# Seven products instead of eight in the first matrix product from block 4 on, with a rewritten instruction list, in a fused retention and MLP kernel

## The chip, the cores and the metric

The kernel runs on one core of a Trainium2 chip. The metric is the device time of one execution in microseconds (us), start to end. The engines are TensorE (PE in the profile, with its weight loads as PEld), VectorE (DVE), ScalarE (ACT), GpSimd (POOL) and SyncE (SP). POOL and SP issue nearly all the transfers here.

## The reference

Inputs: q, k, v of shape (8, 8, 576, 64), that is batch B, heads H, positions S and head width D, and the MLP's weights `w_in` (512 x 2048) and `w_out` (2048 x 512), all float32. First a retention layer without softmax, then a GELU MLP over its 4608 tokens of width 512:

```python
scores = 1/sqrt(D) * q @ k.T                    # per batch and head
gamma  = 1 - 2.0 ** (-5 - arange(H))            # one decay per head
ret    = scores * where(rel >= 0, gamma ** rel, 0)   # rel = query position - key position
x      = (ret @ v) as (B*S, H*D)
out    = gelu(x @ w_in) @ w_out
```

## The kernel before

**Tiling.** The sequence of 576 is cut into four chunks of 128 positions and a tail of 64. A unit is one chunk of one batch; units 0 to 3 are the first chunks of batches 0 to 3, and from there two batches go side by side as a pair, so a group is a pair of units (or the two tails of a pair, in one unit). There are 36 units in 22 groups. For a group, q and k are turned (head width onto the partitions), scores are formed, masked by the decay, and multiplied by v (`inner`); the part from earlier chunks comes through a running state of keys times values (`state`, on the scaled v that `scaled_v` makes) and the turned q (`cross`); `evacuate` writes the result, transposed, into the MLP's input `xT`. Four units make a block of 512 tokens, so there are nine blocks, 0 to 8.

**The MLP.** Its first product for a block is 16 output stripes of 128, each four matmuls of 512 columns, in `mlp1` (line 762). For blocks 5 to 8 it is formed instead by `fast` (line 1021): on a pair of stripes, in four groups j of them, Strassen's method with seven products P1 to P7, each four matmuls of 256 columns (line 1047). The sums that it needs of the weights are made once, by `sum_in` and `sum_last` (the last writes over `w_in` itself, so no plain product may come after it), and those of the input once per block by `sum_x`. P7's product is copied out of PSUM into a tile `p7`, P1's is copied within PSUM, and sums on VectorE join the products. The second product of blocks 1 to 8 is made of seven products too, in `part` (line 948), with sums on VectorE of g and in `after`; block 0's is plain (`mlp2`, line 807).

**Buffers.** q and k of a group lie in one of `N_LD` = 5 load tiles. The turned q and k lie in one of `N_QKT` = 4 tiles; a turn into a tile waits until the cross product of the group four before has read it. The tile `p7` has no place of its own: up to block 6 it lies in the place of the mask `near`, then in a load tile.

**Turning.** `turn` (line 499) turns on TensorE through PSUM, four 128x128 transposes at a time; a full pair needs four such calls. `turn_dma` (line 510) has SP issue a DMA transpose from SBUF to SBUF, two per group. Groups 0 to 6 are turned on TensorE, groups 7 to 21 by DMA.

**The order of the work** is written out by hand in a list `SEQ` (line 1109), which `perform` goes through, and the framework keeps the order per engine. Each entry is a letter and numbers: L is a load (0, 1, 2 for q, k, v of a unit, 3 and 4 for a stripe of `w_in` and `w_out`), t a turn on TensorE, d a turn by DMA, s scores, m masking, i inner, u state, x cross, e evacuate, v scaling, 1 a call of `mlp1`, 2 of `mlp2`, f block.group.product of `fast`, p block.product.quarter of `part`, W, I, J, X and G the sums, K a late store, and w dummy matmuls on zeros that fill TensorE's time. Loads are issued by POOL in list order, at most eight in flight, over its software queue. DMA turns and output stores are issued by SP in list order, so a turn stands behind every store that comes ahead of it in the list, and a store waits for the last sum on VectorE that makes its rows. A planner in the same file keeps due times (`T`, `free_at`, `land`), and chooses by them between VectorE and ScalarE for copies and among PSUM banks; the list itself is fixed.

Of the kernel before, what the change touches and what calls it, by code (L numbers as in the profile page):

```python
# [9 lines left out]
FP32 = mybir.dt.float32  # L10
# [7 lines left out]
def kernel(  # L18
# [52 lines left out]
    FAST, ALL_FAST = 5, 5  # L71
    N_LD = 5
    N_QKT = 4
# [185 lines left out]

    def qk_free(n):  # L260
        g = groups[n]
        ends = list(sg[n]["ends"].values()) if "ends" in sg[n] else [sg[n]["T"]]
        assert len(ends) == 2 or n < N_PE_TR and sg[n]["halves"] == 4
        assert units[g[0]][2] is None or g[0] in s_done
        return max(ends + [st[g[0]].get("U", 0.0)])
# [141 lines left out]
    def pe_waits(until):  # L407
        assert until < 1e8
        T["pe"] = max(T["pe"], until)
# [109 lines left out]
    def scores(n):  # L519
        g = groups[n]  # L520
        qkT = sg[n]["qkT"]
        pe_waits(sg[n]["T"])
# [448 lines left out]
    near_p7 = True  # L971
# [5 lines left out]
    f_bank, f_at, f_done, f_begun, p7_tiles = {}, {}, {}, [], {}  # L977
# [43 lines left out]
    def fast(t, j, p):  # L1021
# [32 lines left out]
        elif p == P7:  # L1054
            late = t >= N_BLK - 2
            if late not in p7_tiles:
                more = {"tag": "qk", "bufs": N_LD} if late else {"tag": "near"}
                p7_tiles[late] = (ld_pool if late else const).tile([128, 2, 2, 256], FP32, name="p7", **more)
            f_bank[key, "p7"] = p7_tiles[late][:, j % 2]
# [45 lines left out]
    for _ in range(N_WARM):  # L1105
# [3 lines left out]
    SEQ = ("L3.1 L1.1 L3.0 L5.0 L0.1 L2.0 L0.2 L1.2 C0.0 C1.0 t0.0.0 Z0 w2 L2.1 Z0 Z1 t0.1.0 Z0 w5 L3.2 Z1 s0 m0 L2.2 Z1 "  # L1109
# [109 lines left out]
```

## Time and profile before

| what | value |
|---|---|
| time, median of 3 runs | 284.95 us (283.55 to 285.13) |
| the profiled execution | 284.17 us, span 282.3 us |
| TensorE busy | 276.3 us, 3413 matmuls |
| VectorE / ScalarE / GpSimd busy | 211.3 / 152.6 / 114.1 us |
| moved by DMA | 35.39 MB, software queue 18.10 MB, hardware queue 16.26 MB |
| output stores (256 KB) | 5.1 us from issue to landing (median) |
| DMA transposes | 30, 7.9 us from issue to landing (median) |

Reading the profile: the first page gives busy time per engine and the span in 40 slices; the chain of work runs backwards from the last instruction; the waits say which engine waited for whom. Matmuls overlap in the record, so a group's time in the chain (start to the next start) is its price, and the mean of one record is not.

### The profile page before, as it was taken

Reading aid. Unit: us, or ns where it says so; the run is one execution under the profiler, and the core shown is the slowest. Engines: PE = TensorE matmul, PEld = TensorE weight load, DVE = VectorE, ACT = ScalarE, POOL = GpSimd, SP = SyncE. Lnnn points to the kernel's source line nnn. Section 1 sums busy time; section 2 is a strip of 40 time slices with the busy share of each in tenths; the row PEclk is TensorE's granted clock in tenths of the full one; section 3 lists DMA queues with packets and bytes.
Section 4 is the critical chain, followed back from the end, with each engine's and each line's share of the span. In section 5 each row is a group of like instructions: output and inputs, shape, how many; then the busy total and the mean of one; then the engine's idle time right before and its main releaser. Section 6 shows DMA issues by size and latency. Waiting matters only on the chain.

```text
span 282.3 us, 8187 instructions
## 1 busy us (share of the span) xinstructions
PE 276.3 (98%) x3413; PEld 211.7 (75%) x3413; DVE 211.3 (75%) x413; ACT 152.6 (54%) x330; POOL 114.1 (40%) x143
## 2 busy tenths in 40 slices
PE   8999999999999999999999999999999999999994
PEld 3576777578874588547775588888888888888894
DVE  5662784886984775989749976898799989984852
ACT  5766745464156631575646565666584457765210
POOL 8987897907955447544076736000000000000000
PEclk9999999999999999999999999999999999999999
DMA  9999999999999999999999999960012013000035
GB/s 146 166 181 179 183 167 178 126 131 202 145 190 177 196 141 127 184 198 138 138 155 138 190 154 156 144 171 1 2 74 77 2 34 120 1 2 0 28 123 150
DMA packets 152804, 35.39 MB, mean 125 GB/s; under 512 B 141120, under 2 KB 148928, under 8 KB 152768
## 3 DMA queue, kind: packets, MB, share of 16 engines
q0 software_dynamic: 116832, 18.10, 101.2%
q1 hardware_dynamic: 34528, 16.26, 32.3%
q10 hardware_dynamic: 1408, 0.52, 0.8%
q8 instruction: 26, 0.43, 0.6%
q14 instruction: 10, 0.08, 0.1%
HBM read 36.70 MB, written 9.44 MB: 163 GB/s over the span
## 4 chain that ended last, share of the span: by engine, by line
PE 91%; POOL 4%; DMA 3%; issue 0%; DVE 0%; POOLq 0%
PE psum L948 35%; PE psum L762 23%; PE psum L1047 18%; PE psum L807 5%; PE psum L651 3%; PE psum L551 3%; DMA w_in<-in_moe_w_in_dram 3%; POOL qk L347 2%; PE psum L702 2%; PE psum L672 1%; POOL v_ld L347 1%; POOL w_in L306 1%; PE psum L499 1%; PE psum L538 0%; PE psum L637 0%
## 5 line engine op out<-in xcount | busy, mean ns | idle before, releaser
L762 PE MATMUL psum<-xT,w_in 128*128 128x512 bf16 (+3 forms) x504 | 74.1, 301 | 0.3 <-DMA w_in<-in_moe_w_in_dram 0.2
L948 PEld LDWEIGHTS <-gs 128*128 128x128 bf16 x656 | 62.3, 98 | 8.3
L771 ACT ACTIVATE g<-psum 128x512 bf16<-128x512 f32 (+2 forms) x91 | 49.6, 546 | 31.6 <-PE psum L762 27.2
L762 PEld LDWEIGHTS <-w_in 128*128 128x128 bf16 x504 | 42.6, 98 | 25.0 <-DMA w_in<-in_moe_w_in_dram 0.9
L948 PE MATMUL psum<-w_sum,gs 128*128 128x256 bf16 (+1 forms) x400 | 50.5, 268 | 0.0
L347 POOL DMA_DIRECT2D qk_ld<-in_k_dram x36 | 30.4, 850 | 29.4 <-DMA qkT<-qk_ld 18.6
L347 POOL DMA_DIRECT2D v_ld<-in_v_dram x40 | 34.3, 865 | 14.0 <-DMA qk_ld<-in_k_dram 5.3
L347 POOL DMA_DIRECT2D qk_ld<-in_q_dram x36 | 30.7, 863 | 15.7 <-DMA qkT<-qk_ld 7.1
L948 PE MATMUL psum<-w_out,gs 128*128 128x256 bf16 x256 | 33.9, 273 | 0.0
L1074 ACT ACTIVATE g<-psum 128x512 bf16<-128x512 f32 x48 | 27.0, 593 | 7.5 <-PE psum L1047 6.5
L948 PE MATMUL psum<-w_sum,g 128*128 128x256 bf16 x256 | 30.8, 273 | 0.0
L948 PEld LDWEIGHTS <-g 128*128 128x128 bf16 x256 | 24.7, 98 | 3.6
L1047 PEld LDWEIGHTS <-w_in 128*128 128x128 bf16 x256 | 24.9, 98 | 3.0
L845 DVE TENSOR_TENSOR gs<-g 128x1024 bf16<-128x1024 bf16 x32 | 21.7, 685 | 3.7 <-ACT g L771 3.1
L849 DVE TENSOR_TENSOR gs<-g 128x1024 bf16<-128x1024 bf16 x32 | 21.6, 684 | 1.4 <-ACT g L771 1.4
L614 ACT ACTIVATE vh<-v_ld,dv 128x64 bf16<-128x64 bf16 x88 | 22.0, 336 | 0.0
L1047 PEld LDWEIGHTS <-wi 128*128 128x128 bf16 x192 | 18.5, 98 | 2.4 <-issue 0.2
L1047 PE MATMUL psum<-xT,w_in 128*128 128x256 bf16 x128 | 19.2, 273 | 0.0
L1047 PE MATMUL psum<-xs,w_in 128*128 128x256 bf16 x128 | 18.9, 273 | 0.0
L1047 PE MATMUL psum<-xs,wi 128*128 128x256 bf16 x128 | 18.7, 273 | 0.0
L617 DVE TENSOR_TENSOR vh<-v_ld,dv 128x512 bf16<-128x512 bf16 x25 | 17.7, 712 | 0.4 <-DMA v_ld<-in_v_dram 0.4
L1070 ACT ACTIVATE g<-p 128x512 bf16<-128x512 f32 x16 | 10.1, 630 | 13.9 <-DVE p L1068 13.9
(101 smaller groups left out, 359.0 us busy)
## 6 DMA issues: line engine op xcount, KB each, us to landing
out_dram<-o SPq DMA_DIRECT2D x27, 256.0 KB, 5.1
v_ld<-in_v_dram POOLq DMA_DIRECT2D x32, 128.0 KB, 7.8
qk_ld<-in_k_dram POOLq DMA_DIRECT2D x28, 128.0 KB, 9.5
qk_ld<-in_q_dram POOLq DMA_DIRECT2D x28, 128.0 KB, 8.3
w_in<-in_moe_w_in_dram POOLq DMA_DIRECT2D x8, 256.0 KB, 7.2
w_out<-in_moe_w_out_dram POOLq DMA_DIRECT2D x8, 256.0 KB, 7.8
out_dram<-o SPq DMA_DIRECT2D x14, 128.0 KB, 2.0
v_ld<-in_v_dram POOLq DMA_DIRECT2D x8, 64.0 KB, 6.7
```

The source lines that it names most:

```text
L347: nc.gpsimd.dma_start(dst, src[2 * bp + jj, :, ci * C:ci * C + n, :].rearrange("h s d -> s h d"))
L614: nc.scalar.activation(vh[:, h, :], loaded[i][1][:, h, :], AF.Copy, scale=dv[:, h, ci:ci + 1])
L617: nc.vector.tensor_tensor(vh, loaded[i][1], dv[:, :, ci:ci + 1].to_broadcast([128, H, D]), op=ALU.mult)
L762: nc.tensor.matmul(hT[:, m, :], lhsT=w[:, cc, o:o + 128], rhs=x_tiles[t][:, cc, lo:hi], start=(cc == 0), stop=(cc == N_DM - 1))
L771: nc.scalar.activation(g_of(t, m0 // 2)[:, m0 % 2:m0 % 2 + n, lo:hi], hT, AF.Gelu)
L807: nc.tensor.matmul(oT, lhsT=g_of(t, m // 2)[:, m % 2, cols], rhs=w_out_sb[m // 2][:, m % 2, :], start=(m == 0), stop=(m == N_DF - 1))
L845: nc.vector.tensor_tensor(s.rearrange("p m a b -> p m (a b)"), g[:, :, 0, :], g[:, :, 1, :], op=ALU.add)
L849: nc.vector.tensor_tensor(s, g[:, :, :, LEFT], g[:, :, :, RIGHT], op=MINUS)
L948: nc.tensor.matmul(m[:, 0 if apart else ts, :], lhsT=a, rhs=w[:, c0:c1], start=p in begins and mm == 0 and ts == 0, stop=mm == N_DF // 2 - ...
L1047: nc.tensor.matmul(m[:, y, :], lhsT=a[:, c], rhs=d[:, c], start=p in (P1, P7) and y == 0 and c == 0, stop=c == 1, skip_group_check=True)
L1070: nc.scalar.activation(g[:, :, 1, RIGHT], v, AF.Gelu)
L1074: nc.scalar.activation(g[:, :, rows, cols], m, AF.Gelu)
```

## The change

1. `FAST` goes from 5 to 4: block 4's first product is made by `fast`, from seven products, and `mlp1` serves blocks 0 to 3.
2. `p7` gets a tile of its own for all blocks (4 KB per partition), and no longer uses the place of `near` or a load tile.
3. `N_QKT` goes from 4 to 3: one tile of 4 KB per partition less.
4. Group 8 is turned on TensorE: four entries t8 in place of two entries d8.
5. The list is another one throughout: 992 entries in place of 977. The loads, the turns and the stores stand in another order, dummy matmuls are 12 in place of 19, and the products of blocks interleave differently.

```diff
-    FAST, ALL_FAST = 5, 5
+    FAST, ALL_FAST = 4, 4
...
-    N_QKT = 4
+    N_QKT = 3
...
+    def turned(n):
+        return len(sg[n].get("ends", ())) == 2 or sg[n].get("halves", 0) == (2 if n < 4 else 4)
+
     def qk_free(n):
...
-        assert len(ends) == 2 or n < N_PE_TR and sg[n]["halves"] == 4
+        assert turned(n)
...
-    near_p7 = True
+    near_p7 = False
...
-            late = t >= N_BLK - 2
-            if late not in p7_tiles:
-                more = {"tag": "qk", "bufs": N_LD} if late else {"tag": "near"}
-                p7_tiles[late] = (ld_pool if late else const).tile([128, 2, 2, 256], FP32, name="p7", **more)
-            f_bank[key, "p7"] = p7_tiles[late][:, j % 2]
+            if not p7_tiles:
+                p7_tiles.append(const.tile([128, 2, 2, 256], FP32, name="p7"))
+            f_bank[key, "p7"] = p7_tiles[0][:, j % 2]
```

Three stretches of the list that the prediction speaks of. The start:

```diff
-"L3.1 L1.1 L3.0 L5.0 L0.1 L2.0 L0.2 L1.2 C0.0 C1.0 t0.0.0 Z0 w2 L2.1 Z0 Z1 t0.1.0 Z0 w5 L3.2 Z1 s0 m0 L2.2 Z1 "
-"w7 L1.3 Z1 t1.0.0 L3.3 Z1 t1.1.0 w2 Z1 i0 L0.3 Z1 v0.0 x0 e0 w2 s1 m1 L2.3 t2.0.0 10.0.2.0.128 L3.4 t2.1.0 "
-"10.2.2.0.128 L3.5 i1 x1 e1 w1 L3.6 s2 m2 10.4.2.0.128 L1.4 10.0.2.128.256 x3 10.2.2.128.256 10.4.2.128.256 "
+"L3.1 L0.1 C0.0 L2.0 C1.0 L1.1 L5.0 Z0 Z0 Z1 t0.0.0 t0.1.0 w3 Z0 s0 m0 Z1 L3.0 Z1 L0.2 L1.2 Z1 Z1 L2.1 w3 "
+"t1.0.0 v0.0 Z1 w1 w1 i0 w3 Z1 e0 t1.1.0 10.2.2.0.128 s1 m1 10.0.2.0.128 w1 L3.2 t2.0.0 t2.1.0 v1.0 i1 e1 s2 "
+"L2.2 u0.0 L3.3 10.0.2.128.256 10.4.2.128.256 10.2.2.128.256 m2 L0.3 i2 e2 10.4.2.0.128 L1.3 10.6.2.0.256 L3.4 "
```

The turns of group 17 (units 27 and 28) and its scores s17, among the two products of block 3 that end in stores (p3.5.3 and p3.6.3):

```diff
-"p3.4.2 d16.0 d16.1 p3.5.0 p3.6.0 d17.0 p3.4.3 p3.5.1 "
-"L2.25 L1.28 p3.5.2 p3.5.3 p3.6.1 i22 J0 i23 L1.31 d17.1 u2.2 v24.1 s15 m24 x14 p3.6.2 v25.0 m25 e22 p3.6.3 "
...
-"L1.29 L1.30 14.15.1.0.512 i26 x16 L0.31 s17 14.14.1.0.512 J4 d18.1 J5 p4.0.0 p4.0.1 p4.0.2 m27 m28 G4.3.1.2 "
+"p3.5.1 d15.0 L1.24 L1.26 L1.25 d15.1 s15 p3.5.2 d16.0 p3.4.2 d16.1 p3.6.1 m24 m25 p3.6.2 L2.25 v25.1 p3.6.3 "
+"p3.4.3 p3.5.3 u2.2 i24 i25 G4.0.1.1 f4.1.0 s16 J5 m26 x15 u2.3 e24 G4.0.1.0 f4.2.0 L0.27 f4.1.1 f4.2.1 f4.1.2 "
+"L2.26 f4.1.3 f4.2.2 f4.3.0 f4.2.3 f4.1.4 f4.2.4 f4.1.5 v26.0 f4.3.1 e25 f4.3.2 f4.2.5 f4.1.6 f4.3.3 G4.0.1.2 "
+"i26 L0.28 x16 f4.2.6 f4.3.4 G4.1.1.1 G4.2.1.1 p4.0.0 p4.0.1 d17.0 f4.3.5 e26 f4.3.6 X5 p4.1.0 L1.27 L1.28 "
+"d17.1 p4.1.1 s17 m27 p4.1.2 m28 f5.0.0 p4.0.2 G4.3.1.1 p4.0.3 f5.0.1 f5.0.2 G4.1.1.0 f5.0.3 f5.1.0 f5.1.1 "
```

More of the change, by code (lines that the diff above doesn't have):

```diff
@@ L521, in scores @@
         qkT = sg[n]["qkT"]
+        assert turned(n)
         pe_waits(sg[n]["T"])
@@ L975, in late_p7 @@
         return not near_p7 or t >= N_BLK - 2
-    f_bank, f_at, f_done, f_begun, p7_tiles = {}, {}, {}, [], {}
+    f_bank, f_at, f_done, f_begun, p7_tiles = {}, {}, {}, [], []
     def sum_in(mm):
@@ L1108 @@
     release(b, T["pe"])
-    SEQ = ("L3.1 L1.1 L3.0 L5.0 L0.1 L2.0 L0.2 L1.2 C0.0 C1.0 t0.0.0 Z0 w2 L2.1 Z0 Z1 t0.1.0 Z0 w5 L3.2 Z1 s0 m0 L2.2 Z1 "
[61 rows of a table removed]
-           "p8.5.0 p8.5.1 p8.5.2 p8.5.3 p8.6.0 p8.6.1 p8.6.2 p8.6.3").split()
+    SEQ = ("L3.1 L0.1 C0.0 L2.0 C1.0 L1.1 L5.0 Z0 Z0 Z1 t0.0.0 t0.1.0 w3 Z0 s0 m0 Z1 L3.0 Z1 L0.2 L1.2 Z1 Z1 L2.1 w3 "
[61 rows of a table added]
+           "p8.4.2 p8.2.3 p8.5.0 p8.4.3 p8.6.0 p8.5.1 p8.5.2 p8.5.3 p8.6.1 p8.6.2 p8.6.3").split()
     def late_store():
```

111 rows, old and new, of the table SEQ are left out of this document.

## The prediction

> **What bounds the kernel now.** I read the page's first two parts, then TensorE's waits, then stages, then the chain of work in order of time. First the page:
>
> ```profile
> span 282.3 us, 8187 instructions
> ...
> PE 276.3 (98%) x3413; PEld 211.7 (75%) x3413; DVE 211.3 (75%) x413; ACT 152.6 (54%) x330; POOL 114.1 (40%) x143
> ...
> PE   8999999999999999999999999999999999999994
> ...
> PEclk9999999999999999999999999999999999999999
> DMA  9999999999999999999999999960012013000035
> ```
>
> TensorE is busy in every slice at full clock, and the transfers are dense up to two thirds of the span. All waits of TensorE over 0.1 us (us in total, times, longest), and two stages (length, then busy time of PE, PEld, DVE, ACT, POOL):
>
> ```profile
> PE psum L1106 <- DVE zeros L119: 1.2, 1, 1.2
> PE psum L499 <- DMA qk<-in_q_dram: 0.7, 1, 0.7
> PE psum L672 <- DVE vh L617: 0.2, 1, 0.2
> PE psum L762 <- DMA w_in<-in_moe_w_in_dram: 0.2, 1, 0.2
> ```
>
> ```profile
> 22.00:50.00 28.00, 28.00 (x365) 20.25 (x363) 17.31 (x39) 16.06 (x37) 22.72 (x28) 1.00 1.98 175
> ...
> 130.00:170.00 40.00, 40.00 (x501) 29.09 (x500) 31.37 (x62) 22.48 (x58) 20.37 (x25) 1.00 1.87 154
> ```
>
> So after the first 21 us TensorE never waits: the time is start-up, then the sum of TensorE's work, then 3.6 us of last stores (282.3 less the end of the last row below). Work taken off TensorE is time gained, and every wait that the new list brings is time lost at full price. The chain (start, length) prices the work:
>
> ```profile
> 51.02 0.45 PE psum L499 x8
> ...
> 137.97 1.73 PE psum L762 x8
> ...
> 206.89 3.49 PE psum L1047 x32
> ...
> 225.67 0.37 PE psum L538 x16
> ...
> 263.31 15.34 PE psum L948 x156
> ```
>
> A transpose costs 0.45/8 = 0.056 us, a matmul of 512 columns 1.73/8 = 0.216, one of 256 columns 3.49/32 = 0.109.
>
> **The change part by part.** *TensorE's work.* Block 4 loses 16 x 4 = 64 matmuls of 512 columns (13.84) and gains 4 groups x 7 products x 4 = 112 of 256 (12.21). Group 8 gains 16 transposes (0.90). Scores, inner, state, cross and the second product keep their counts. Net **-0.73 us**. The Trainium skill ("TensorE: Matmul & The Clock Gate", Part 4: PE-mode transpose) puts such a transpose at about 275 ns inside a kernel; by that figure the 16 would cost 4.4 us, and the sum would come out 3.5 us higher. Here the row decides against it, 8 in 0.45 us, since they follow each other as matmuls do.
>
> *Start-up.* TensorE's first steps, and the load that they hang on:
>
> ```profile
> 1.19 4.44 PE L1106 MATMUL psum<-zeros 128*128 128x512 bf16 x10 [1.19 <-DVE zeros L119]
> ...
> 13.98 0.41 PE L651 MATMUL psum<-ret,v_ld 128*64 128x128 bf16 x8
> 14.33 0.39 PE L1099 MATMUL psum<-zeros 128*128 128x512 bf16 x1
> ...
> 17.33 0.41 PE L672 MATMUL psum<-vh,qk 128*64 128x64 bf16 x15 [0.24 <-DVE vh L617]
> ...
> 21.05 1.47 PE L762 MATMUL psum<-xT,w_in 128*128 128x384 bf16 x8 [0.24 <-DMA w_in<-in_moe_w_in_dram]
> ```
>
> ```profile
> 7.66 0.91 POOL L347 DMA_DIRECT2D v_ld<-in_v_dram  x1
> ```
>
> The step at 13.98 is `inner` of unit 1, which needs that unit's v, the eighth load of POOL's queue in both lists. Ahead of it both lists have the same useful work, so 6 of the 7 dummy matmuls left out (0.216 each) buy nothing: waits take their place. I keep this step at 14.0. Behind it, before loses one dummy (0.22) and the two waits of 0.24; after has no dummy, and I expect two short waits of 0.1 to 0.2 for a copy and a scaling. Net -0.5, rounded with what a wait hides in the record. From there the new list asks for the next w_in, q and k some 0.3 to 0.9 us after I expect them (a load of 128 KB takes 0.8 us at the 165 GB/s between the last columns of the two stage rows, and the fifth w_in stands 14th in the queue in place of 15th). So the term is **-0.5**, from -1.0 (all losses gone) to +0.9 (one load late).
>
> *Group 17's turns.* Both turns stand behind all four stores of block 3 on SP now; before, one stood ahead of them and one behind two. How that went before, with the landing of the one at 145.81 (its median in the second fence), and of three turns that went in a train:
>
> ```profile
> 144.16 0.69 DVE L897 SCALAR_TENSOR_TENSOR o<-psum,o 128x512 f32<-128x512 f32 x1 [3.29 <-PE psum L948]
> 144.88 0.81 SPq L789 DMA_DIRECT2D out_dram<-o  x2
> 145.81 2.26 SPq L510 DMA_TRANSPOSE qkT<-qk_ld  x1
> ```
>
> ```profile
> L510 SPq DMA_TRANSPOSE qkT<-qk_ld x1: 2257/2257/2257, 145.8 to 145.8; - x1
> ...
> DMA to landing us min/median/max: 9.2/9.2/9.2
> ```
>
> ```profile
> L510 SPq DMA_TRANSPOSE qkT<-qk_ld x3: 1200/1325/4131, 95.1 to 97.8; - x3
> ...
> DMA to landing us min/median/max: 7.0/9.5/10.4
> ```
>
> ```profile
> 36.35 0.64 PE L651 MATMUL psum<-ret,vh 128*64 128x128 bf16 x16
> ...
> 37.52 1.47 PE L807 MATMUL psum<-w_out,g 128*128 128x512 bf16 x6
> ...
> 158.91 0.32 PE L637 MATMUL psum<-ret,vh 64*64 64x64 bf16 x16
> ...
> 159.19 0.63 PE L551 MATMUL psum<-qkT 64*64 64x128 bf16 x32
> ```
>
> The scores of group 17 began at 159.19, 4.2 us after the turn landed (145.81 + 9.2). In the new list the last quarter of block 3's M6 (p3.5.3) is followed, up to these scores, by 25 product entries (25 x 0.436 = 10.9), two inner, a state and a cross (37.52 - 36.35 = 1.17), the tail's scores (0.37), its inner and cross (159.19 - 158.91 = 0.28) and another state (about 0.34, its share of the 1.17): 13.1 us. In that time come the VectorE sum and two stores (144.16 to 145.81, and an estimate of 0.1 between the product's last matmul and the sum: 1.75), a first turn (9.2 after its issue), the second about 3.05 behind it (the three of the train landed at 102.1 to 108.2) and, as an estimate from the two stores more ahead of it, 0.5: 14.5. So TensorE waits **+1.4**. Bounds: 0, if the second needs 9.2 from its own issue 1.3 later (12.3); +3.0, if turn and stores space out by the longest times seen (1.75 + 10.4 + 3.05 + 0.9). While TensorE waits, everything behind it waits, since its queue is in order.
>
> *Group 10's turns* had the least room, and lose some:
>
> ```profile
> L510 SPq DMA_TRANSPOSE qkT<-qk_ld x2: 1331/2742/4152, 82.2 to 83.7; - x2
> ...
> DMA to landing us min/median/max: 9.3/10.1/10.9
> ```
>
> ```profile
> 95.93 0.64 PE L551 MATMUL psum<-qkT 64*64 64x128 bf16 x32
> ```
>
> Landed at 94.6 (83.7 + 10.9), needed at 95.9: 1.3 of room. The new list has 0.9 us less useful work ahead of these scores, start-up is 0.5 shorter, and the last load that the turns need is the 64th transfer in place of the 62nd (1.6 later). Against that stand group 8's two turns, gone from the same queue (3.05 each at most). Room: 1.3 - 0.9 - 0.5 - 1.6 = -1.7 without the relief, +4.4 with all of it; group 11's are like it. I take **+0.4**, bounds 0 and +2.0.
>
> *At nothing.* The third tile less: group n's turn waits for the cross of group n-3, which stands well ahead in the list; the load or the store ahead of it comes later. Group 10's first turn would be the one to feel it, with x7 right ahead of it in the list; its second turn waits longer, for the 64th transfer, and if that came early the cost stays within the 2.0 above. VectorE and ScalarE get block 4's copies and sums:
>
> ```profile
> L1064 DVE TENSOR_TENSOR psum<-p,psum 128x512 f32<-128x512 f32 x16 | 11.1, 692 | 4.7 <-PE psum L1047 2.3 <-ACT p L474 2.1
> L1068 DVE TENSOR_TENSOR p<-p,psum 128x512 f32<-128x512 f32 x16 | 10.8, 683 | 3.4 <-PE psum L1047 3.3
> L1009 DVE TENSOR_TENSOR xs<-xT 128x512 bf16<-128x512 bf16 x8 | 3.0, 418 | 0.0
> ```
>
> Four groups with four such 0.69 us steps and four input sums of 0.42 make 12.7 us; between 130 and 170 us the two engines have 80 - 31.4 - 22.5 = 26 us free, and half of the steps are copies that either can take. The GELUs keep their number of elements. The tile of its own only takes waits away.
>
> *The sum:* -0.73 - 0.5 + 1.4 + 0.4 = **+0.6**. On the profiled execution of 284.17 us (1.9 around its span) that is 284.8; the three runs' median is 284.95, 0.8 above it, so I forecast 285.5 for a median.
>
> **The rivals.** *All turns land in time.* For it: nothing after 21 us waits now, and two turns fewer share the DMA. Against it: room that was 1.3 to 4.2 is spent in two places. It gives -0.73 - 0.5, or 283.7, and 283.2 with start-up at its best.
>
> *Slower: the loads collide with the turns.* The turns of groups 15 and 16, when landed, set free load tiles, and some ten loads then start beside group 17's turns. It decides from the point where the second turn lands over 13.1 us after p3.5.3. At the upper bounds (3.0 and 2.0, start-up at 0) the sum is +4.3, or 289.2; at 2.5 and 1.2 it is +2.5, or 287.4. For it: turns that took 9.2 to 10.9 with loads beside them. Against it: those three kinds of row scatter by 2 us about their middle, not by 4.
>
> *The clock falls in the start-up.* The first ten dummies took 4.44, that is 0.44 each, twice 0.216: a half clock exists at the start. With dummies left out, TensorE might fall back to it; the same 4.4 us of it lose 2.2 and give 287.7. Against it: the gaps are under 1 us each. The Trainium skill ("TensorE: Matmul & The Clock Gate", Part 1: The HAM clock gate) has the clock fall only after an idle window of about 3.4 us; by that rule it does not happen, and the full clock in all slices of before agrees.
>
> *VectorE becomes the bound of block 4's stage*, if copies pile up on it: of the 12.7 us it would take 8.6 free ones first, and some 4 would show: 289.
>
> **How the numbers follow.** Forecast (285.5, its own range 284.0 to 287.0): 0.42. All in time (283.7): 0.25. Collision (287.4 to 289.2): 0.25. Clock 0.04, VectorE 0.04. Half a per cent, about what a measurement can tell here, is 1.4 us, so faster means under 283.5 and slower over 286.4. Faster 0.20 (most of the second case); same 0.42 (0.37 of the forecast, 0.05 of the second); slower 0.38 (0.05 of the forecast, the rest of the cases). The range 283.0 to 289.0 leaves out about 0.1 on each side.
>
> **What would show it.** Work: TensorE's groups at line 762 lose 64 of the 504, those of 256 columns gain 112, at the same prices. Start-up: `inner` of unit 1 near 14.0 us, then hardly a wait up to 35 us. Turns: a wait of TensorE at line 555 (the scores; 551 before) for a DMA into qkT near 160 us of about 1.4, and perhaps a small one near 94 to 104. Wrong if no such wait shows, if one over 3 us does, if the clock row falls, or if waits for VectorE show between 140 and 170 us.

## The result, and the profile after

| | before | after |
|---|---|---|
| median of 11 runs each (lowest to highest) | 284.76 us (283.55 to 288.22) | 288.71 us (285.43 to 291.29) |
| ratio, 95% interval | | 1.010 (1.006 to 1.014) |
| profiled execution, its span | 284.17, 282.3 us | 286.89, 285.0 us |
| the same kernels on a second chip, median (23 and 12 runs) | 284.78 us | 286.82 us, ratio 1.006 (1.004 to 1.008) |

The changed kernel is slower: by 1.0% on the first chip, by 0.6% on the second. Executions more than 1.5% above their kernel's fastest are left out of the ratios, though not of the medians. The forecast of 285.5 was no change; the time lies inside the range of 283.0 to 289.0, near its upper end.

The page after; each digit of the third line is TensorE's busy share in one fortieth of the span, the last line is the chain that ended last:

```profile
span 285.0 us, 8286 instructions
...
PE 274.2 (96%) x3456; PEld 217.1 (76%) x3470; DVE 215.9 (76%) x417; ACT 155.2 (54%) x317; POOL 114.2 (40%) x143
...
PE   7999999999999799998999899999999999999994
...
PEclk9999999999999999999999999999999999999999
...
PE 70%; DMA 20%; POOL 5%; issue 1%; DVE 1%; SPq 0%; ACT 0%; POOLq 0%; DVEq 0%
```

TensorE's busy time fell and the span grew: three slices in the middle are no longer full. What TensorE waited for (us in total, times, longest), and the three places in order of time; in brackets the idle time ahead of the row:

```profile
PE psum L555 <- DMA qkT<-qk_ld: 3.3, 3, 1.4
PE psum L1108 <- DVE zeros L119: 1.2, 1, 1.2
```

```profile
95.57 0.64 PE L555 MATMUL psum<-qkT 64*64 64x128 bf16 x32 [1.38 <-DMA qkT<-qk_ld]
...
135.42 0.64 PE L555 MATMUL psum<-qkT 64*64 64x128 bf16 x32 [0.68 <-DMA qkT<-qk_ld]
...
164.33 0.64 PE L555 MATMUL psum<-qkT 64*64 64x128 bf16 x32 [1.27 <-DMA qkT<-qk_ld]
```

These are the scores of groups 10, 14 and 17. All three wait for a turn of q or k. Where SP issued those turns (start, length, count of a run of equal instructions), in three answers of the timeline:

```profile
81.33 2.59 SPq L793 DMA_DIRECT2D out_dram<-o  x4
84.02 3.53 SPq L513 DMA_TRANSPOSE qkT<-qk_ld  x1
```

```profile
117.62 3.57 SPq L793 DMA_DIRECT2D out_dram<-o  x5
121.35 16.48 SPq L513 DMA_TRANSPOSE qkT<-qk_ld  x6
149.63 2.03 SPq L793 DMA_DIRECT2D out_dram<-o  x4
151.82 9.51 SPq L513 DMA_TRANSPOSE qkT<-qk_ld  x3
```

Each of the three waits hangs on a turn that SP issued right after a run of output stores (L793). The last two of these runs had themselves stood waiting for VectorE's sums (7.2 and 11.7 us); the first stood behind group 10's first turn, which had waited until 79.5 for its tile, that is for group 7's cross product (ended at 79.4). The turn at 84.02 landed 11.5 us later, at 95.53; the ones at 122.81 (the second of its run) and 153.69 landed 12.6 and 10.6 later, at 135.38 and 164.28. TensorE resumed within 0.05 us of each landing.

Group 17's turns have been moved behind their stores, as the prediction's rows of before show. Those of groups 10 and 14 stood behind the same stores before, and TensorE did not wait for them then:

```profile
75.04 7.04 SPq L789 DMA_DIRECT2D out_dram<-o  x4
82.25 7.91 SPq L510 DMA_TRANSPOSE qkT<-qk_ld  x3
...
111.88 5.80 SPq L789 DMA_DIRECT2D out_dram<-o  x5
117.85 5.80 SPq L510 DMA_TRANSPOSE qkT<-qk_ld  x2
```

The difference of the two profiled executions, 2.7 us, adds up so:

| term | forecast | measured | from |
|---|---|---|---|
| TensorE's work | -0.73 | -0.7 | plain block 4 without stores costs 1.62 (below), less 16 transposes at 0.056 |
| start-up | -0.5 | -0.9 | useful work done by 40 us: 14 matmuls of 256 columns more than before, 2 of 512 and 4 transposes fewer, at the prediction's prices |
| group 17's scores | +1.4 | +1.3 | the row at 164.33 |
| groups 10 and 11 | +0.4 | +1.4 | the row at 95.57; none at group 11 |
| group 14's scores | 0 | +0.7 | the row at 135.42 |
| last matmul to the end | 0 | +0.5 | 3.7 before, 4.1 after |
| sum | +0.6 | +2.3 | |

0.4 us are left over. The other 1.8 us up to the median of 288.71 are not in this execution; most of the runs that make them have a lower granted clock, below.

### The profile page after: what moved, and what is told of

The parts are those of the page before. It is cut to its first block, busy times and chain, and to the rows that moved or that the text cites. A ratio compares the mean times of both kernels' runs of the same rounds, so it can differ in the third digit from the quotient of the medians.

```text
span 285.0 us, 8286 instructions
## 1 busy us (share of the span) xinstructions
PE 274.2 (96%) x3456; PEld 217.1 (76%) x3470; DVE 215.9 (76%) x417; ACT 155.2 (54%) x317; POOL 114.2 (40%) x143
## 4 chain that ended last, share of the span: by engine, by line
PE 70%; DMA 20%; POOL 5%; issue 1%; DVE 1%; SPq 0%; ACT 0%; POOLq 0%; DVEq 0%
PE psum L952 28%; PE psum L1051 19%; PE psum L766 11%; DMA qkT<-qk_ld 11%; DMA qk_ld<-in_k_dram 7%; PE psum L811 4%; DMA w_in<-in_moe_w_in_dram 3%; PE psum L555 2%; PE psum L655 2%; POOL qk L350 2%; POOL w_in L309 2%; PE psum L502 1%; POOL v_ld L350 1%; PE psum L676 1%; PE psum L706 1%
## 5 line engine op out<-in xcount | busy, mean ns | idle before, releaser
L766 PE MATMUL psum<-xT,w_in 128*128 128x128 bf16 (+3 forms) x433 | 59.8, 289 | 1.1 <-DMA w_in<-in_moe_w_in_dram 0.2
L775 ACT ACTIVATE g<-psum 128x512 bf16<-128x512 f32 (+2 forms) x75 | 39.8, 535 | 29.9 <-PE psum L766 25.9
L1076 ACT ACTIVATE g<-psum 128x512 bf16<-128x512 f32 x60 | 34.2, 594 | 13.0 <-PE psum L1051 12.9
L1051 PEld LDWEIGHTS <-wi 128*128 128x128 bf16 x240 | 23.3, 98 | 2.9
L1051 PE MATMUL psum<-xs,wi 128*128 128x256 bf16 x160 | 23.5, 273 | 0.0
L1051 PE MATMUL psum<-xT,w_in 128*128 128x256 bf16 x160 | 23.4, 273 | 0.0
L1051 PE MATMUL psum<-xs,w_in 128*128 128x256 bf16 x160 | 23.4, 273 | 0.0
L592 DVE TENSOR_TENSOR ret<-psum,msk 128x1024 bf16<-128x1024 f32 x17 | 20.3, 1218 | 3.6 <-PE psum L555 3.0
L1072 ACT ACTIVATE g<-p 128x512 bf16<-128x512 f32 x20 | 12.6, 631 | 13.3 <-DVE p L1070 13.2
L621 DVE TENSOR_TENSOR vh<-v_ld,dv 128x512 bf16<-128x512 bf16 x29 | 19.5, 684 | 0.0
```

Of the source, the lines that this page charges most:

```text
L592: nc.vector.tensor_tensor(r.rearrange("p e h q -> p (e h) q"), both_of(got[0][0], HP), by, op=ALU.mult)
L621: nc.vector.tensor_tensor(vh, loaded[i][1], dv[:, :, ci:ci + 1].to_broadcast([128, H, D]), op=ALU.mult)
L766: nc.tensor.matmul(hT[:, m, :], lhsT=w[:, cc, o:o + 128], rhs=x_tiles[t][:, cc, lo:hi], start=(cc == 0), stop=(cc == N_DM - 1))
L775: nc.scalar.activation(g_of(t, m0 // 2)[:, m0 % 2:m0 % 2 + n, lo:hi], hT, AF.Gelu)
L1051: nc.tensor.matmul(m[:, y, :], lhsT=a[:, c], rhs=d[:, c], start=p in (P1, P7) and y == 0 and c == 0, stop=c == 1, skip_group_check=True)
L1072: nc.scalar.activation(g[:, :, 1, RIGHT], v, AF.Gelu)
```

## The experiments

The order theory: the scores wait because the turns stand behind output stores in SP's queue. The traffic theory: the turns are late because the transfers of that time fill the DMA engines, in whatever order they are issued. Beside them the question of the clock: the changed kernel's runs spread over 6 us, and most of the longer ones show a mean granted clock under 0.995. (The mean also takes in the end of the span, where TensorE is done and a low clock costs it nothing. This alone made 0.995 in one profiled execution, that with only block 3's stores moved: its last matmul ended at 282.6, half clock began at 284.9.) Each kernel's runs stand against runs of the kernel before on the same chip, whose medians were 284.55 to 284.78.

**The changed kernel again.**

> The changed kernel again, unaltered, as the base of the comparisons on this chip. Its profile showed 286.9 us with waits of TensorE of 1.45, 0.74 and 1.44 us at the scores of groups 10, 14 and 17, at a granted clock of 1.000; its median of 11 runs was 288.7, with clocks of 0.986 to 1.000. Order theory (the scores wait for DMA turns that stand behind output stores in SP's queue) and traffic theory (they wait because the transfers of that time fill the DMA engines, in whatever order they are issued) both say: the same three waits again, 3.0 to 4.0 us in sum. Clock theory: a wait of over a microsecond lets the granted clock fall, at some executions more than at others, so the runs scatter from 285.4 to 291.3 and those of lower clock are the longer ones; if the profile catches one, the clock is low in the slices behind a wait. Its rival: the clock falls at random or in the start-up, with no relation to the waits.

Measured: 286.82 (284.94 to 290.08). The same turns are waited for, 2.9 us in sum, the longest (1.6) at group 17; the wait at group 14 is down to under 0.3:

```profile
PE psum L555 <- DMA qkT<-qk_ld: 2.9, 3, 1.6
```

Ten of the twelve runs had a clock of 0.997 or more; their median is 286.5, and that of the first chip's five such runs 286.46. The other two here, 289.85 and 290.08, had 0.990 and 0.985. So at full clock the change costs 1.7 us on both chips.

**Stores off SP, held together.** For blocks 1 to 3:

```diff
+        if 0 < t < 4:
+            held_stores.append([12, lambda: store_now(t, ts, src, lo, hi, nc.scalar, nc.scalar)])
+            return
...
     for x in SEQ:
+        for one in held_stores:
+            one[0] -= 1
+        while held_stores and (held_stores[0][0] <= 0 or x[0] == "p" and x.endswith(".0.0")):
+            held_stores.pop(0)[1]()
         perform(x[0], [int(y) for y in x[1:].split(".") if y])
```

> The changed kernel, with the stores of blocks 1 to 3 issued 12 list entries later, by ScalarE's queue, so that no turn stands behind them in SP's queue; the bytes are the same, some 3 to 6 us later. Order theory: the second turn of groups 10 and 17 lands 3 to 5 us earlier after its issue, the three waits (3.6 us in sum) fall below 0.5 in sum, and the time is 283.5 to 285 at full clock, 1.5 to 3.4 us under the changed kernel. Traffic theory: turns still need 9 to 12 us to land and at least 2.5 us of waits stay; time within 1 us of the changed kernel. Clock theory: with the waits gone the granted clock is 0.998 or more in every run and the scatter shrinks to about 1.5 us, so the median falls by more than the waits (up to 5 us); if the clock has nothing to do with the waits, the scatter stays at 4 to 6 us.

Measured: 288.48 (287.26 to 289.8), ratio 1.012 (1.009 to 1.016). The three waits for turns are gone, as the order theory has it, and one new wait has taken their place:

```profile
PE psum L960 <- ACT xT L477: 3.4, 1, 3.4
```

ScalarE's timeline shows why:

```profile
120.73 4.69 ACTq L801 DMA_DIRECT2D out_dram<-o  x3
125.46 1.07 ACT L477 CAST xT<-psum 128x512 bf16<-128x512 f32 x2 [4.24 <-DVE ret L600]
```

Three store issues took 4.69 us of ScalarE's queue, the copy into xT behind them came late, and TensorE stood. (The row names a VectorE step that ended together with the third issue, at 125.42; the run with spaced stores below tells the two apart.) Its granted clock (the column before the DMA share) then fell to a half, in the middle of the wait, and stayed there until 131.6:

```profile
122.80:124.80 2.00, 0.00 (x0) 0.00 (x0) 1.93 (x6) 0.00 (x0) 2.00 (x4) 1.00 2.07 164
124.80:126.00 1.20, 0.00 (x0) 0.00 (x0) 0.61 (x2) 0.54 (x2) 1.20 (x2) 0.51 1.48 166
126.00:131.60 5.60, 5.50 (x16) 2.16 (x16) 2.62 (x7) 2.72 (x6) 1.84 (x3) 0.50 1.34 204
131.60:133.60 2.00, 2.00 (x38) 1.19 (x36) 0.00 (x0) 1.19 (x2) 0.00 (x0) 0.99 1.59 136
```

So a wait of 3.4 us cost another 2.8 (half of the 5.5 us from its end, at 126.1, to 131.6). I had expected at most 285, since I gave the moved issues no price on ScalarE.

**Stores left out.**

```diff
     def store(t, ts, src, lo=0, hi=d_model, *on_queues):
+        if 0 < t < 4:
+            return
```

> The changed kernel without the output stores of blocks 1 to 3 (their rows of the output are not written, 3 MB less to transfer). Order theory: nothing stands ahead of the turns, the waits at groups 10, 14 and 17 are gone, 283 to 284.5 us, equal to the kernel with held stores within 0.7. Traffic theory: only this kernel loses the waits, the one with held stores does not, so they differ by 2 us or more. If the q and k loads themselves are late (a third theory), the waits stay here too, over 2 us in sum.

Measured: 284.2 (283.25 to 284.42), ratio 0.997 (0.996 to 0.998); all 12 runs at a clock of 0.997 or more. The chain is TensorE's again:

```profile
PE 92%; POOL 2%; DMA 2%; issue 1%; DVE 0%; ACT 0%; POOLq 0%
```

No wait at the scores is left, with three tiles of turned q and k and with block 4's copies and sums on VectorE and ScalarE. So neither of these two costs TensorE anything by itself. Group 17's turns were issued at 141.7 and 143.0 here, ten us sooner, and landed 3.5 and 4.6 later, in place of 9.4 and 10.6. So leaving the stores out also shortens the flight, and this run alone cannot tell order from traffic; the one before it, with the same bytes, and the next can.

**The order alone, in the kernel before.** Its list, with nothing else of the change:

```diff
-p3.5.0 p3.6.0 d17.0 p3.4.3 p3.5.1 L2.25 L1.28 p3.5.2 p3.5.3 p3.6.1 i22 J0 i23 L1.31 d17.1 u2.2 v24.1 s15 m24 x14 p3.6.2 v25.0 m25 e22 p3.6.3
+p3.5.0 p3.6.0 p3.4.3 p3.5.1 L2.25 L1.28 p3.5.2 p3.5.3 p3.6.1 i22 J0 i23 L1.31 u2.2 v24.1 s15 m24 x14 p3.6.2 v25.0 m25 e22 p3.6.3 d17.0 d17.1
```

> The kernel before, with one edit of its list: both turns of group 17 moved behind the last store of block 3, as they stand in the changed kernel. No fast product is added. Order theory: issued at about 152 in place of 138 and 146, the turns land at about 161 and 164.3 as in the changed kernel (9.4 and 10.6 us after their issue), the scores are ready at 159.2, so TensorE waits some 5 us: 287.5 to 290.5 us. Traffic theory: with the loads of the kernel before, the turns land 3 to 5 us after their issue and the time moves by less than 1.5 us. Clock theory: the kernel before then shows runs with a granted clock under 0.995 as well, 1 to 4 us longer than the wait alone explains; without it, all runs stay at 0.998 to 1.000.

Measured: 293.18 (292.03 to 294.94), ratio 1.030 (1.027 to 1.033). The wait is where the order theory puts it, 6.3 us against the 5 expected:

```profile
PE psum L551 <- DMA qkT<-qk_ld: 6.3, 1, 6.3
```

The turns were issued at 153.15 and 156.16 and landed 10.7 and 10.9 later. The rest is the clock, at a half from the middle of the wait to 173.2:

```profile
160.80:162.80 2.00, 0.00 (x0) 0.00 (x0) 0.79 (x3) 0.25 (x1) 0.68 (x1) 1.00 2.36 150
163.20:167.20 4.00, 0.08 (x4) 0.08 (x8) 0.00 (x0) 0.00 (x0) 0.68 (x1) 0.50 1.66 128
167.20:173.20 6.00, 6.00 (x52) 3.67 (x53) 3.98 (x5) 0.60 (x1) 2.35 (x4) 0.50 1.90 148
173.20:175.20 2.00, 2.00 (x21) 1.78 (x19) 0.00 (x0) 1.74 (x7) 1.64 (x2) 1.00 1.75 143
```

All six runs had a clock of 0.988 or less. The order of two turns alone, with the loads of the kernel before, brings a wait at group 17, and a longer one than in the changed kernel; the traffic theory had given it under 1.5 us.

**Half of that dose.** Only d17.1 goes behind p3.6.3; d17.0 stays.

> The kernel before with a smaller dose of the same edit: only the second turn of group 17 moves, from ahead of the last two stores of block 3 to behind them, from 145.8 to about 152. Order theory: it lands some 9 to 10.5 us later, at 161 to 162.5, the scores are ready at 159.2, so TensorE waits 1.8 to 3.3 us, about half of the run with both turns moved (6.3); time 286.5 to 288 at full clock. Clock theory: after a wait of 6.33 and after one of 3.35 us the granted clock stood at 0.50 to 0.60 for some 6 to 8 us, after one of 1.6 us it did not move; here, between these, some of the runs should show a clock of 0.995 or less and some 0.998 or more, and the former should be 2 to 4 us longer than the latter. Its rival, that the clock loss grows with the wait: all runs show a small loss of 1 us or so.

Measured: 289.0 (287.16 to 291.2), ratio 1.016 (1.012 to 1.019). The wait was 2.0 us in the profiled execution, at full clock:

```profile
163.41 0.64 PE L551 MATMUL psum<-qkT 64*64 64x128 bf16 x32 [2.04 <-DMA qkT<-qk_ld]
```

Three of six runs had a clock of 0.987 to 0.994 and a median of 289.88, the other three 288.43. Some runs lose the clock and some don't, as expected at a wait of this length, but they differ by 1.5 us and not by 2 to 4. The full-clock runs are 0.4 above what I had expected; in the profiled one two early waits, for a load of w_in (1.2) and for a VectorE step (0.6), stand beside it, at places where this list is that of the kernel before.

**Stores off SP, one at a time.** As in the run with held stores, but 5 entries after the data and then one every 3 entries:

```diff
-            held_stores.append([12, lambda: store_now(t, ts, src, lo, hi, nc.scalar, nc.scalar)])
+            held_stores.append([5, lambda: store_now(t, ts, src, lo, hi, nc.scalar, nc.scalar)])
...
+        if held_stores and held_stores[0][0] <= 0:
+            held_stores.pop(0)[1]()
+            for one in held_stores:
+                one[0] = max(one[0], 3)
```

> The changed kernel with the stores of blocks 1 to 3 on ScalarE's queue again, but one at a time: the first 5 list entries after its data, each next one 3 entries later. With the stores held together three of five store issues in a row took 4.69 us of ScalarE's queue at 120.7 us, its copies came late and TensorE waited 3.35 us. If a run of stores fills the queue (its issue waits for transfers), spacing them takes that wait away: no wait over 0.6 us is left, clock 0.997 or more in every run, 283.8 to 285.2 us, which is the kernel without those stores (284.2) within 1.0. If the stores cost TensorE through traffic as such, at least 1.5 us of waits stay and the time is 285.7 or more.

Measured: 291.01 (289.32 to 292.53), ratio 1.020 (1.017 to 1.023): the expectation was wrong. ScalarE stood still between the fourth store of block 2 and the fifth:

```profile
121.81 0.60 ACT L775 ACTIVATE g<-psum 128x512 bf16<-128x512 f32 x1 [0.82 <-PE psum L555]
129.35 0.34 ACTq L801 DMA_DIRECT2D out_dram<-o  x1
129.73 1.07 ACT L477 CAST xT<-psum 128x512 bf16<-128x512 f32 x2 [7.33 <-DMA qkT<-qk_ld]
```

```profile
PE psum L960 <- ACT xT L477: 6.8, 1, 6.8
```

No full queue: the releaser is a turn. SP had run ahead and issued group 14's first turn at 118.53; it landed at 129.33, and the store was issued at 129.35. In the trace both carry the same semaphore, and the store waits for the turn's landing before it uses that again. With held stores the fifth store did the same (issued at 125.09, the turn landed at 125.06), so it was this in both runs. It is a new wait that my edit made, and no word on the traffic theory: the waits for turns were gone.

**Plain products for block 4, in the new list.**

```diff
-f4.0.0 v23.0 p3.4.1 p3.3.0 f4.0.1 p3.3.1 p3.2.3 f4.0.2 f4.0.3
+14.0.1.0.512 v23.0 p3.4.1 p3.3.0 p3.3.1 p3.2.3 14.1.1.0.512
...
-        return max(at, f_at[(t - 1, j + 2), "V"]) if t > FAST and (late_p7(t) == late_p7(t - 1)) else at
+        return max(at, f_at[(t - 1, j + 2), "V"]) if t > FAST + 1 and (late_p7(t) == late_p7(t - 1)) else at
```

> The changed kernel, list and all, with block 4's first product by plain products of 512 columns at the places of its fast ones (its weights have been summed by then, so block 4's values are not the reference's). TensorE gets 13.84 - 12.21 = 1.63 us more work, nearly all of it ahead of group 17's scores. If the saved work is given back as a wait (order theory): the wait at those scores shrinks by about as much as the work grows, and the time moves by -0.3 to +0.6 against the changed kernel (286.8), so 286.5 to 287.4. If the saved work counts in full: +1.3 to +1.9, 288.1 to 288.7.

Measured: 287.49 (286.4 to 288.44), 2.86 above the kernel before on its chip; the changed kernel stood 2.04 above it on its own. So the plain products cost 0.82 here, or 1.1 against the changed kernel's runs at full clock (1.7 above), more than the 0.6 expected at most and less than the 1.63 counted. The interval of the ratio, 1.007 to 1.013, is 1.6 us wide, so the six runs do not settle it.

> The same plain block 4 with the stores of blocks 1 to 3 left out as well (their rows of the output are not written), where the changed kernel had no waits left (284.2). Both theories: without a wait to absorb it the work counts in full, 284.2 + 1.6 = 285.8, from 285.4 to 286.2. Less than +0.8 would mean that the count of TensorE work (64 matmuls of 512 columns against 112 of 256) is wrong as a price.

Measured: 285.67 (285.6 to 286.81), 1.04 above the kernel before on its chip, where the kernel without stores stood 0.58 below it on its own: 1.62 in all, for 1.63 counted. So the saving of the fast product is real. With the stores in place 0.8 to 1.1 of it reached the time. That the rest came back as waiting for turns fits the profile (0.6 us of it, where the changed kernel had 1.6 to 3.3), but the times do not settle it:

```profile
PE psum L555 <- DMA qkT<-qk_ld: 0.6, 2, 0.4
```

**Stores of blocks 1 and 3 off SP, and an earlier quarter of block 7.** As with held stores, with `if t in (1, 3):` and 4 entries in place of 12, and in the list:

```diff
-p8.1.3 p8.2.0 p8.2.1 p8.2.2 G8.3.1.0 p8.3.0 p8.3.1 G8.2.1.1 p8.3.2 G8.2.1.2 p8.3.3 p8.4.0 p7.5.3 G8.3.1.2
+p8.1.3 p7.5.3 p8.2.0 p8.2.1 p8.2.2 G8.3.1.0 p8.3.0 p8.3.1 G8.2.1.1 p8.3.2 G8.2.1.2 p8.3.3 p8.4.0 G8.3.1.2
```

> The changed kernel with the stores of blocks 1 and 3 alone on ScalarE's queue, 4 list entries later (block 2's stay on SP, since its fifth store waited there for a turn to land), and with the last quarter of block 7's M6 (p7.5.3) ten entries earlier, as in the list before. Order theory: the waits at groups 10 and 17 (1.45 and 1.44) are gone, one of 0.7 to 1.2 us at group 14 stays; with the earlier quarter block 7's last stores are out of the way and the stretch from the last matmul to the end falls from 4.1 to 3.7 us: 283.8 to 285.2, level with the kernel before or up to 0.9 under it, at a clock of 0.996 or more in every run. Traffic theory: the waits come back elsewhere, 286 or more.

Measured: 285.8 (284.82 to 286.67), ratio 1.003 (1.000 to 1.006), all 12 runs at 0.996 or more: 1.25 us above the kernel before, where the changed kernel stood 2.04 above it (1.7 at full clock); 0.6 over the upper end of what I had expected. Waits for turns fell to one of 0.8:

```profile
81.34 0.64 PE L555 MATMUL psum<-qkT 64*64 64x128 bf16 x32 [0.75 <-DMA qkT<-qk_ld]
```

It is not the expected one at group 14, whose turns still stood behind block 2's five stores (issued at 120.54 and 122.34) and came in time. It stands at the scores of group 9, whose second turn left SP at 69.55, with no store issued since 52.07, and took 11.7 us to land. So a turn can also come late by its flight alone.

```profile
142.44 5.11 SPq L513 DMA_TRANSPOSE qkT<-qk_ld  x2
```

Group 17's turns left SP at 142.44 and 143.78 in place of 151.82 and 153.69, landed at 150.7 and 155.6, and nothing waited. Their flight was no shorter (8.3 and 11.8 us against 9.4 and 10.6); they were only issued ten us sooner. The second half of the edit failed: from the last matmul to the end it took 4.7 us, not 3.7, so block 7's quarter is not what lengthens the tail.

**Only block 3's stores off SP.** The same with `if t in (3,):` and the list as it was.

> The changed kernel with only block 3's four stores on ScalarE's queue, 4 list entries later: one wait undone. Order theory: the wait at group 17's scores goes (its turns no longer stand behind these stores), those at groups 10 and 14 stay (1.45 and 0.74), so 1.2 to 1.6 us less than the changed kernel at full clock: 285.2 to 285.8; runs with a lowered clock become fewer than in the changed kernel (8 of 23 at 0.994 or less) but do not vanish. Traffic theory: the wait at group 17 stays over 1 us and the time is 286.4 or more.

Measured: 287.67 (285.76 to 293.26), ratio 1.009 (1.005 to 1.012), a miss: no gain. The wait at group 17 is gone. Those at groups 10 and 14 stayed (2.3 us together), one of 0.6 came up at group 11, and the four issues stood in ScalarE's queue for 2.76 us, so that a product of block 4 waited for the copy behind them. Three of twelve runs had a clock of 0.994 or less, against 7 of the changed kernel's 23 (the 8 above is a miscount):

```profile
151.93 2.76 ACTq L801 DMA_DIRECT2D out_dram<-o  x4
```

```profile
155.86 0.60 PE L1059 MATMUL psum<-xs,w_in 128*128 128x256 bf16 x4 [1.12 <-ACT u_sb L477]
```

**Two more profiled executions of the changed kernel.**

> The changed kernel unaltered, one look, to catch an execution in which the granted clock is low. Clock theory: if its mean clock is 0.994 or less, one of the waits at groups 10, 14 and 17 is longer than the 1.6 us seen at full clock (2 us or more), and the low clock stands in the slices right behind that wait; at 0.997 or more all waits are 1.7 us or shorter. Rival: the low clock stands elsewhere (in the start-up, or without a wait ahead of it).

> As the look before it, a second execution of the unaltered changed kernel: same expectations (low clock right behind a wait of 2 us or more, or no wait over 1.7 us and a clock of 0.997 or more).

Measured: 287.0 at a clock of 0.996, and 285.84 at 1.000. The waits, first execution and second:

```profile
PE psum L555 <- DMA qkT<-qk_ld: 2.8, 2, 2.1
```

```profile
PE psum L555 <- DMA qkT<-qk_ld: 1.6, 2, 1.0
```

The first one's wait of 2.1 at group 17 left the clock full; only the last slice of the span is below. So four executions of one kernel have waits of 1.6 to 3.3 us at these places. An execution of the changed kernel with the clock down in mid-kernel was not caught.

## Why the prediction was right or wrong

- **What bounds the kernel: right.** Work on TensorE counted in full where nothing waited (1.62 for 1.63), and so did the waits.
- **TensorE's work: right**, -0.7 for -0.73.
- **Start-up: mis-sized, for the better.** I kept `inner` of unit 1 at 14.0, "the eighth load of POOL's queue in both lists". It came 0.8 earlier (13.2 to 13.5 in the other three traces of this kernel). I had misread the row of before: no wait stands ahead of it, v had landed at 13.59, and dummies filled the time, so the load did not hold it. After, v landed at 13.10 and `inner` followed at once:

```profile
13.14 0.49 PE L655 MATMUL psum<-ret,v_ld 128*64 128x128 bf16 x8 [0.23 <-DMA v_ld<-in_v_dram]
```

- **Group 17's turns behind block 3's stores: right, place and size.** +1.4 forecast, 1.3 measured, 0.6 to 2.1 in the other three traces of this kernel. Moving the same two turns in the kernel before makes the wait (6.3 us), taking the stores off SP unmakes it.
- **Group 10: the mechanism was right, the term mis-sized**, +0.4 for 1.4 (0.7 to 1.1 in the other three). I set the relief from group 8's two turns against lost room, and the relief did not show. The second turn stood behind four stores before as well and was issued only 0.3 later (84.02 for 83.68), where I had counted 1.6 for its load. But it took 11.5 us to land, 0.6 longer than any that I had used, and TensorE came for it at 94.19, 1.7 sooner than before, where I had counted 1.4. So part of what the start-up won was lost again here.
- **Group 14: the step that was missing.** I costed the turns behind the stores for groups 10, 11 and 17 only, and put group 14 at nothing without a reason. Group 14's turns stood behind block 2's five stores before too, and the second landed 2.5 us before its scores (130.35 and 132.87). In the new list it was issued 3.3 later (122.81 for 119.46), took 12.6 us in place of 10.9, and was wanted only 1.9 later, at 134.74: a wait of 0.7 in this execution, 0.2 or less in the other three.
- **At nothing:** the third tile and VectorE's 12.7 us cost nothing by themselves, as the kernel without stores shows. With the stores the tile can have up to 0.4 us of group 10's wait, as an estimate: the four stores left at 81.33, behind the turn that waited for the tile, though VectorE had made the last of their rows by 80.91. No run tests this apart. The tail was not at nothing: +0.5. Of it 0.34 lies between the last matmul and the last store's issue (0.46 before, 0.80 after); what moved it was not found.
- **The rivals.** Collision is the nearest: 287.4 to 289.2 for 288.71. But its cause, loads beside the turns, is not what decided; the same loads with sooner turns do no harm. The flight of a turn does vary, from 3.0 us to 12.6 in one execution, and was shorter without the stores, so traffic has a share that the runs do not size. The clock rival was put in the wrong place. I dismissed a fall in the start-up, and there was none; I did not ask what a wait in mid-kernel does to the clock.
- **The range and the chances.** That the first chip's median lies in the range is in part luck: its upper end came from the collision, and 1.8 us of the way to 288.71 lie outside every term. The likeliest outcome, no change (0.42), did not come; slower (0.38) did. At full clock the time, 286.5, lies in the forecast's own range of 284.0 to 287.0.

That clock is the last step, and the one that the sum lacked. At full clock the changed kernel takes 286.5, +1.7; on the first chip six of eleven runs had 0.996 or less, and they lift the median. What is shown: waits of 3.4, 6.3 and 6.8 us pull the clock down, two to three us after their beginning, and the kernels whose longest wait of TensorE after 21 us was 0.8 or less in the profile (no stores, plain block 4 with and without stores, blocks 1 and 3 off SP) had no run under 0.995 in 41. The kernel before, which hardly waits, had one in the 62 beside the experiments (0.994). The kernel with a wait of 2.0 had three in six. What is only argued: that in the changed kernel's long runs the wait at group 10 or 17 grew past two us, since there is no trace of such a run. Nor does the clock explain all of it: if the share that it lacks is taken off the span of those six runs, 286.1 to 289.1 us are left, where the five at full clock took 285.4 to 286.9.

No version tried beats the kernel before and still writes the whole output.

## What to carry to other kernels

In an in-order queue the price of a transfer is not its flight alone but also what it is queued behind: a store that waits for a sum holds back every turn after it, and moving the store to a compute engine's queue can move the wait there. Go through every transfer that a new order puts behind a store, not only those with the least room, and also through those that stood behind it already, since an earlier need or a later store uses up their room. And count a wait of TensorE of two us or more at up to nearly double its length (3.4 us cost another 2.8 here), because the clock can fall with it.

## What the runs showed that I had not expected

- TensorE's clock fell 2.1 us after it stopped in the run with held stores (stopped at 122.75, half clock from 124.81), 2.2 in the kernel before with late turns, 2.8 with spread stores, and stayed at a half for 6.8, 10.2 and 6.8 us (read in windows of 0.4 us). The Trainium skill ("TensorE: Matmul & The Clock Gate", Part 1: The HAM clock gate) lets it fall after an idle window of about 3.4 us, free-running. The lengths at half clock are close to two, three and two such windows, but the fall came before a full one had passed; here the measurement decides. The clock's changes lie whole steps of 3.41 us apart in these traces (157.0 us, 46 steps, from the rise at 133.16 to the fall at 290.18, behind the last matmul, with spread stores; 119.5 us, 35 steps, from 173.20 to 292.67 with late turns). Each of the three falls ended a step in which TensorE had stood for 2.1, 2.2 and 2.8 us. The waits of 2.04 and 2.10 us that left the clock full lay across two steps, with at most 1.9 and 1.2 us in one. So by these five traces what matters is how much of one step a wait fills, and a wait of just over two us can go either way.
- A DMA can wait for another one on a different queue through a shared semaphore: 7.3 us of ScalarE for a turn that SP had issued.
- The 19 turns that SP issued between 70 and 165 us took 3.0 to 12.6 us to land in one execution of the changed kernel, so its median is a poor bound.
